# Attention with top-k masking and a routed MoE on one core: the gate's weights copied by ScalarE, and five constant tables moved to PSUM

## The chip, the cores and the metric

The kernel runs on one core of a Trainium2 chip. A core has five engines with queues of their own: TensorE (PE, matrix products and transposes), VectorE (DVE), ScalarE (ACT), GpSimd (POOL) and SyncE (SP, which here only issues DMAs). Each works through its instructions in the order of the program and waits on semaphores where it needs another's result. The metric is the device time of one execution in microseconds; less is better. SBUF is the working memory; PSUM holds 8 banks of 512 fp32 words in each of 128 partitions, and is where PE writes.

## The reference

The first part is attention in which each row keeps its 32 greatest scores, the second a mixture of eight experts, one per token:

```python
scores = scale * np.matmul(q, k.transpose(0, 1, 3, 2))          # B=8, H=8, S=576, D=64
kth = np.partition(scores, -32, axis=-1)[..., -32:-31]
scores = np.where(scores >= kth, scores, -1000000000.0)
attn = softmax(scores);  attn_out = np.matmul(attn, v)
x = attn_out.transpose(0, 2, 1, 3).reshape(B * S, H * D)        # 4608 tokens of 512

logits = x @ w_gate                                             # 8 experts
expert_idx = np.argmax(logits, axis=1)
gate_w = softmax(logits)[arange(N), expert_idx]
for e in range(8):                                              # each token goes to one expert
    out[mask_e] = gate_w[mask_e] * (np.maximum(x[mask_e] @ w1[e], 0) @ w2[e])
```

All inputs and the output are fp32.

## The kernel before

**Attention** runs over 144 steps `t` (line 1005 on), 18 for each of the 8 batches. A step handles two tiles of 128 query rows by 576 keys. The work on one pair of tiles is spread over several steps, and each pass of the loop issues, in this order:

- ACT: the exponentials of step t-4 (`exps`, line 468), which read the transposed scores from the PSUM tile `three` (named `tt`);
- ACT and POOL: the mask of step t-2 (`softmax`, lines 455 and 456): ACT writes the sign of score minus threshold, and POOL adds it to the scores so that masked ones vanish in the exponential;
- PE and ACT: the scores of step t+3 (`scores`, `scores_left`, lines 367 to 388) into PSUM, and their copy to SBUF (`sb`), from where SP also stores them to HBM (line 403);
- PE: the product with v of step t-5 (`av`, lines 478 and 493) and the transposes of step t-3 into `tt` (`transp`, line 462), nine chunks of 128 columns;
- DVE: the top-k of step t (`topk`): 21 MAX8 over pieces of the two tiles (line 1026) and then rounds of MAX8 and MATCH_REPLACE8 on the candidates (line 1034). POOL makes the thresholds `nb` of it (line 1008).

Beside this run small jobs, written as generators: `j_prep` (transposes of q and k), `j_sums`, `j_rows` (token rows and partial logits), `j_find` (rows whose mask kept a wrong number), `j_redo` and `j_patch` (these rows again) and `j_route` (expert and place of each token). They don't issue at once: `pe`, `act`, `vec` and `pool` (line 265 in the profile) put their instructions into four lists, `pq`, `aq`, `dq` and `gq`. A planner (`advance`, with costs from `need` and due times from `DUE`) decides at the end of each step which job goes on. PE's and ACT's lists are flushed in the next step ahead of the top-k; DVE's is flushed in the second half of the top-k, one job instruction behind each instruction of line 1034.

PSUM is full while attention runs: three banks for `tt` (of which the transposes use 1152 of 1536 columns), two for the scores, one (`px`) for the product with v and odd pieces, two for the jobs (`bank`, named `pt`). When attention ends (`att_open[0] = False`), all but the last two go to the MoE.

The tile framework sets the semaphores. Places that matter here: the prologue (lines 980 to 993) ends with two DVE copies that put the gate's weights `wg` into columns 128 to 143 of `turner`, the moving matrix with which `j_rows` turns token rows (first needed at step 14). `wg` comes by a DMA on SP's queue (line 129). Five constant tables in SBUF feed small DVE instructions: `level` (in `settle`, the softmax shifts), `idx1` (`j_find`, key), `slots` (`j_find`, `r_sl` and `r_qx`), `edesc` and `valid` (`j_route`).

**The MoE** (line 1084 on) gathers the tokens of an expert, splits them and the weights into two fp32r parts each, and multiplies on PE (lines 1154 and 1169). It starts with four experts' first tokens as soon as batch 4 is routed; the routes of the last batches run beside it.

Of the kernel before, what the change touches and what calls it, by code (L numbers as in the profile page):

```python
# [8 lines left out]
F32 = mybir.dt.float32  # L9
# [4 lines left out]
AF = mybir.ActivationFunctionType  # L14
OP = mybir.AluOpType
# [7 lines left out]
TOPK = 32  # L23
# [25 lines left out]
def attention_moe(ctx, tc, q, k, v, w_gate, w1, w2, out):  # L49
    nc = tc.nc  # L50
    B, H, S, D = q.shape
    HP = H // 2
    DM = H * D
    E = w_gate.shape[1]
# [17 lines left out]
    KB = MAIN + 1  # L72
# [23 lines left out]
    psum = att.enter_context(tc.tile_pool(name="psum", bufs=1, space=PSUM))  # L96
# [22 lines left out]
    turner = consts.tile([128, HP, RW], F32, name="turner")  # L119
# [8 lines left out]
    wg = consts.tile([128, DC, E], F32, name="wg")  # L128
# [6 lines left out]
    edesc = consts.tile([128, KB, E], F32, name="edesc")  # L135
    nc.gpsimd.iota(edesc, pattern=[[0, KB], [-1, E]], base=E, channel_multiplier=0,
                   allow_small_or_imprecise_dtypes=True)
    valid = consts.tile([128, KB, E], BF, name="valid")
# [3 lines left out]
    hist = consts.tile([128, E, 2 * KB + 1], BF, name="hist")  # L142
# [7 lines left out]
    idx1 = consts.tile([128, NLT], F32, name="idx1")  # L150
    nc.gpsimd.iota(idx1, pattern=[[1, NLT]], base=1, channel_multiplier=0, allow_small_or_imprecise_dtypes=True)
    slots = consts.tile([128, 128], BF, name="slots")
# [8 lines left out]
    stat = consts.tile([128, B, 3], F32, name="stat")  # L161
# [6 lines left out]
    for i in range(3):  # L168
        t = consts.tile([128, S], BF, name=f"sg{i}")
# [24 lines left out]
    level = consts.tile([128, 3], F32, name="level")  # L194
# [18 lines left out]
    for p in range(HP):  # L213
        for h in range(2):
# [3 lines left out]
            a = attr[:, t0:t0 + 2 * MAIN - 1:2, :]  # L218
# [4 lines left out]
            a = attr[h * LEFT:(h + 1) * LEFT, tl_, :]  # L223
# [8 lines left out]
    for i in range(3):  # L232
        t = work.tile([128, 2, KW], F32, name=f"qk{i}", bufs=1)
# [11 lines left out]
    for i in range(2):  # L245
        t = jobs.tile([128, NLT + 1, 2], F32, name=f"nb{i}", bufs=1)
# [3 lines left out]
    for i in range(NV):  # L250
        t = jobs.tile([128, 2, VW], F32, name=f"rv{i}", bufs=1)
# [5 lines left out]
    VQ, CNT, NB = {}, {}, {}  # L257
# [4 lines left out]
    cell, held, att_open = [1], [0], [True]  # L262

    def later(queue):
        return lambda f, *a, **k: queue.append(lambda: f(*a, **k))  # L265

    pe, act, vec, pool = later(pq), later(aq), later(dq), later(gq)
# [8 lines left out]
    def need(**k):  # L276
        return k

    def flush(queue):
        while queue:  # L280
            queue.pop(0)()
# [15 lines left out]
    def bank():  # L297
        return free.pop(0)

    NB9 = 2 * MAIN + 1  # L300
    three = psum.tile([128, NB9 * 128], F32, name="tt")

    MAINS = psum.tile([128, 2, 512], F32, name="ps")

# [132 lines left out]
    def spread(pt):  # L437
        pe(nc.tensor.matmul, pt[:, 0:128], top.to_broadcast([128, 128]), ident, start=True, stop=True)

    def settle(pt, ns, done):  # L440
        mm = jobs.tile([128, 1], F32, name="mm")
        vec(nc.vector.tensor_reduce, mm, pt[:, 0:128], axis=AX.X, op=OP.max)
        vec(done)
        k = len(ns)
        vec(nc.vector.scalar_tensor_tensor, shift[:, ns[0]:ns[0] + k], slope[:, None, :].to_broadcast([128, k, 3]), mm,
            level[:, None, :].to_broadcast([128, k, 3]), op0=OP.mult, op1=OP.add)

    SHIFTED = {0, 1, 2, 3}

# [165 lines left out]
    def j_find(b):  # L615
        sm = lambda name, shape, dt=F32: jobs.tile(shape, dt, name=name, bufs=1)
        yield need(dve=0.3)
        while (b + 1) * NLT // (2 * NT) - 1 not in CHECKED:
            yield
        key = sm("r_key", [128, NLT])  # L620
        vec(nc.vector.scalar_tensor_tensor, key, CNT[b], float(2 * TOPK - S), idx1, op0=OP.not_equal, op1=OP.mult)
        vec(nc.vector.max, rhs[:, :, 0], key)
        ok = sm("r_ok", [128, 9], BF)
        vec(nc.vector.tensor_scalar, ok[:, 0:8], rhs[:, :, 0], 0.0, None, op0=OP.is_gt, op1=OP.add,
            accum_out=ok[:, 8:9])
        nbb = NBB[b % 2]
        ntab = dram.tile([128 * (NLT + 1), 2], F32, name=f"ntab{b}")
        nc.sync.dma_start(ntab.rearrange("(p t) a -> p t a", p=128), nbb)
        yield need(spot=1, pe=0.1)
        pr, leave = spot("stat")  # L630
        pe(nc.tensor.matmul, pr[:, 0:1], before, ok[:, 8:9], start=True, stop=True)
        pe(nc.tensor.matmul, pr[:, 1:3], ones, ok[:, 7:9], start=True, stop=True)
        act(nc.scalar.activation, stat[:, b], pr[:, 0:3], AF.Copy)
        if 2 * b + 4 < NQ:
            spread(pr[:, 128:256])
            settle(pr[:, 128:256], [2 * b + 4, 2 * b + 5], leave)
            SHIFTED.update([2 * b + 4, 2 * b + 5])
        else:
            act(leave)
        yield need(slack=1)  # L640
        yield need(dve=1.3)
        sl = sm("r_sl", [128, 8], BF)
        vec(nc.vector.scalar_tensor_tensor, sl, slots[:, 0:8], stat[:, b, 0:1], ok[:, 0:8], op0=OP.add, op1=OP.mult)
        oh = sm("r_qx", [128, 512]).bitcast(BF).rearrange("p (j x) -> p j x", j=8)
        vec(nc.vector.tensor_tensor, oh, slots[:, None, :].to_broadcast([128, 8, 128]),
            sl[:, :, None].to_broadcast([128, 8, 128]), op=OP.is_equal)
        yield need(spot=1, pe=0.5)
        pl, leave = spot("li")
        for j in range(8):
            pe(nc.tensor.matmul, pl[:, 0:2], oh[:, j], rhs[:, j], start=(j == 0), stop=(j == 7))  # L650
        li = sm("r_li", [128, 2])
        act(nc.scalar.activation, li, pl[:, 0:2], AF.Copy)
        act(leave)
        yield need(slack=1)
        yield need(dve=0.1)
        fl = sm("r_fl", [128, 1], I32)
        vec(nc.vector.tensor_scalar, fl, li[:, 1:2], float(NLT + 1), li[:, 0:1], op0=OP.mult, op1=OP.add)
        yield need(pool=2.0)
        at = sm("r_at", [128, 4], I32)
        pool(nc.gpsimd.indirect_dma_start, out=at, out_offset=None, in_=atab,  # L660
             in_offset=bass.IndirectOffsetOnAxis(ap=fl[:, 0:1], axis=0))
        nb = jobs.tile([128, 8], F32, name="r_nb", bufs=3)
        pool(nc.gpsimd.indirect_dma_start, out=nb[:, 0:2], out_offset=None, in_=ntab,
             in_offset=bass.IndirectOffsetOnAxis(ap=fl[:, 0:1], axis=0))
        yield need(pool=1.8)
        qi = jobs.tile([128, 2], I32, name="r_qi", bufs=3)
        pool(nc.gpsimd.tensor_scalar, qi, at[:, 0:3:2], b * H * S, None, op0=OP.add)
        sb = jobs.tile([128, S], F32, name="r_sb", bufs=2)
        pool(nc.gpsimd.indirect_dma_start, out=sb, out_offset=None, in_=SCD[b],
             in_offset=bass.IndirectOffsetOnAxis(ap=at[:, 0:1], axis=0))  # L670
        hf = sm("r_hf", [128, 1])
        pool(nc.gpsimd.tensor_copy, hf, at[:, 1:2])
        hm = jobs.tile([128, H], F32, name="r_hm", bufs=3)
        pool(nc.gpsimd.tensor_scalar, hm, eight, hf, None, op0=OP.is_equal)
        hmb = hm[:, :, None].to_broadcast([128, H, D])
        pool(nc.gpsimd.tensor_scalar, used[:, b:b + 1], hf, float(H), None, op0=OP.is_lt)
        yield need(pool=0.7)

        low = nb[:, 2:3]
        pool(nc.gpsimd.tensor_scalar, nb[:, 3:4], nb[:, 1:2], 1.0 + 2.0 ** -10, None, op0=OP.mult)  # L680
        pool(nc.gpsimd.tensor_scalar, low, nb[:, 0:1], -(2.0 ** -7), None, op0=OP.mult)
        pool(nc.gpsimd.tensor_tensor, low, low, nb[:, 3:4], op=OP.add)
        FOUND[b] = (sb, nb, qi, hmb)
# [106 lines left out]
    def j_route(b):  # L790
# [14 lines left out]
        sh = small("sh", [128, KB, E])  # L805
        ex = small("gex", [128, KB, E])
        oh = small("oh", [128, KB, E])
# [2 lines left out]
        vec(nc.vector.tensor_reduce, lg, ll.rearrange("p i (h e) -> p i e h", h=H), axis=AX.X, op=OP.add)  # L810
        vec(nc.vector.tensor_reduce, mx, lg, axis=AX.X, op=OP.max)
        vec(nc.vector.tensor_tensor, sh, lg, mx[:, :, None].to_broadcast([128, KB, E]), op=OP.subtract)
        vec(nc.vector.scalar_tensor_tensor, oh, sh, 0.0, edesc, op0=OP.is_equal, op1=OP.mult)
        vec(nc.vector.tensor_reduce, fm, oh, axis=AX.X, op=OP.max)
        vec(nc.vector.tensor_tensor, oh, oh, fm[:, :, None].to_broadcast([128, KB, E]), op=OP.is_equal)
        yield need(dve=0.6)
        vec(nc.vector.tensor_tensor, hist[:, :, KB + 1:].rearrange("p e c -> p c e"), oh, valid, op=OP.mult)
        win = bass.AP(hist.tensor, hist.offset, [list(hist.ap[0]), list(hist.ap[1]), [1, KB + 1], [1, KB + 1]])
        vec(nc.vector.tensor_reduce, cum, win, axis=AX.X, op=OP.add)
        vec(nc.vector.tensor_copy, hist[:, :, KB], cum[:, :, KB])  # L820
# [22 lines left out]
        for c in range(KB):  # L843
            if c == 0 or b not in ahead or b == part_of[0][0]:
                yield need(pool=1.0)
            n = 128 if c < MAIN else LEFT
# [142 lines left out]
            for queue in (gq, pq, aq, dq):  # L989
                flush(queue)  # L990
    drain()
    for h in range(2):
        nc.vector.tensor_copy(turner[h * D:(h + 1) * D, :, 128 + h * E:128 + (h + 1) * E], wg[h * D:(h + 1) * D])
    nc.sync.dma_start(xs[0:PAD, :], zero[:, 0:DM])
    nc.sync.dma_start(atab.rearrange("(p t) a -> p t a", p=128), attr)
    for i in range(B):
# [8 lines left out]
    for t in range(steps + LAG + TD + 4):  # L1005
        n, s = divmod(t, NT)
# [26 lines left out]
        for m, (f, a) in enumerate(two):  # L1033
            f(*a)  # L1034
            if mine and m >= 2:
                mine.pop(0)()
        flush(mine)
        if t == 0:
            nc.vector.tensor_reduce(top, VQ[0][:, 0:2, 0], axis=AX.X, op=OP.max)
            first_pt = bank()  # L1040
            spread(first_pt)
            pq.pop()()
# [401 lines left out]
    n = over(moe_a, counts, cap, otab, lambda: next(g))  # L1444
# [50 lines left out]
```

## Time and profile before

| | us |
|---|---|
| median of 3 runs (lowest, highest) | 1278.51 (1277.42, 1278.90) |
| profiled execution: its own time | 1278.04 |
| profiled execution: its span, first to last instruction | 1276.2 |
| busy in the span: PE, DVE, POOL, ACT | 1209.7, 1020.9, 840.1, 832.6 |
| mean granted clock of PE | 0.988 |

A row of the timeline gives start, duration (us), engine, line, operation, output and inputs by the program's names, partitions x elements, and how many like it follow one another; in brackets stands the idle time of the engine before it and what ended this. PE is TensorE's matmuls, PEld its weight loads, SPq the DMAs that SP issues. Instructions of the small jobs all have line 265, so one goes by the tiles. A group's row gives count and durations of all instructions of one kind. The row of a stretch gives, for each engine, busy time and number of instructions, then the granted clock, the busy share of the DMA engines and GB/s.

### The profile page before, as it was taken

How to read it: one execution, taken by the hardware profiler on the slowest of the kernel's cores; microseconds unless marked ns; L12 is line 12 of the kernel's file. 1: busy time of each engine (PE TensorE's matmuls, PEld its weight loads, DVE VectorE, ACT ScalarE, POOL GpSimd, SP SyncE). 2: the span in 40 equal slices, each digit the busy share in tenths (PEclk: the TensorE clock that was granted, in tenths of full speed). 3: DMA queues.
4: the chain of work that ended last, by engine and by line, in shares of the span. 5: the costliest groups of instructions: out<-in, count | busy, mean ns of one | idle time of the engine just before them, and what ended most of it. 6: DMA issues, size and time to landing. Idle time of an engine off the chain costs nothing.

```text
span 1276.2 us, 31656 instructions
## 1 busy us (share of the span) xinstructions
PE 1209.7 (95%) x9126; PEld 963.3 (75%) x9126; DVE 1020.9 (80%) x6898; ACT 832.6 (65%) x1699; POOL 840.1 (66%) x1213
## 2 busy tenths in 40 slices
PE   6999999999999999999999879899999999999997
PEld 3667667766676767666667668789899998899996
DVE  7999999999999999999999986755674333446555
ACT  4999798998898898898998853333333232333433
POOL 4676666767977967967968858766554242455654
PEclk8999999999999999999999999899999999999999
DMA  6765564654655655665654635745665243556773
GB/s 172 233 179 184 165 204 145 191 180 154 190 177 165 196 169 167 194 176 164 187 172 144 184 101 147 223 125 173 167 192 162 75 135 93 155 164 193 228 213 112
DMA packets 276758, 215.37 MB, mean 169 GB/s; under 512 B 136617, under 2 KB 218713, under 8 KB 276576
## 3 DMA queue, kind: packets, MB, share of 16 engines
q1 hardware_dynamic: 265840, 190.11, 50.5%
q0 software_dynamic: 9504, 22.86, 5.7%
q8 instruction: 74, 1.21, 0.4%
q14 instruction: 108, 0.88, 0.2%
q10 hardware_dynamic: 1232, 0.30, 0.1%
HBM read 106.69 MB, written 107.90 MB: 168 GB/s over the span
## 4 chain that ended last, share of the span: by engine, by line
DVE 43%; PE 42%; ACT 5%; POOL 4%; issue 3%; DMA 2%; SPq 1%; POOLq 0%; ACTq 0%; DVEq 0%
DVE cand L1026 21%; PE ph L1154 17%; PE y L1169 17%; DVE cand L1034 9%; DVE vq L1034 8%; PE pt L265 2%; ACT sg L455 2%; POOL sb L456 2%; PE mt L1134 1%; PE px L478 1%; PE ps L367 1%; DVE xm L265 1%; POOL wl L958 1%; PE tt L462 1%; ACT sb L369 1%
## 5 line engine op out<-in xcount | busy, mean ns | idle before, releaser
L456 POOL TENSOR_TENSOR sb<-sb,sg 128x576 f32<-128x576 f32 x288 | 370.1, 1302 | 48.3 <-ACT sg L455 41.1
L1026 DVE MAX8 cand<-sb 128x8 f32<-128x52 f32 (+2 forms) x3024 | 366.3, 207 | 0.0
L958 POOL TENSOR_TENSOR wl<-r,wh 128x512 fp32r<-128x512 f32 x118 | 153.2, 1299 | 207.2 <-DVE wh L957 201.8
L455 ACT ACTIVATE sg<-sb,nb 128x576 int8<-128x576 f32 x288 | 229.0, 795 | 49.5 <-POOL sb L456 48.9
L1155 ACT ACTIVATE hh<-ph 128x256 fp32r<-128x256 f32 (+3 forms) x136 | 58.4, 429 | 247.6 <-PE ph L1154 247.5
L478 PEld LDWEIGHTS px<-et,rv 128*64 128x64 f32 x2688 | 129.9, 137 | 119.0 <-ACT xt L265 47.6
L1034 DVE MAX8 vq<-cand 128x8 f32<-128x22 f32 (+7 forms) x1152 | 200.5, 205 | 0.0
L367 PE MATMUL ps<-qk 64*128 64x512 f32 (+1 forms) x576 | 185.0, 650 | 3.9 <-ACT sb L369 3.2
L462 PE MATMUL tt<-turner,sb 128*128 128x128 f32 x1296 | 173.5, 276 | 14.8 <-POOL sb L456 10.4
L1156 DVE SCALAR_TENSOR_TENSOR hl<-ph,hh 128x256 fp32r<-128x256 f32 (+3 forms) x136 | 65.0, 478 | 150.8 <-ACT hh L1155 150.5
L468 ACT ACTIVATE et<-tt,shift 128x1152 f32<-128x1152 f32 x144 | 178.4, 1239 | 2.9 <-PE tt L462 2.9
L478 PE MATMUL px<-et,rv 128*64 128x128 f32 (+1 forms) x2688 | 163.1, 267 | 11.4 <-ACT xt L265 8.7
L1154 PE MATMUL ph<-xh,wh 128*128 128x256 f32 (+3 forms) x536 | 169.8, 317 | 0.0
L1154 PE MATMUL ph<-xh,wl 128*128 128x256 f32 (+3 forms) x536 | 165.8, 309 | 0.0
L1154 PE MATMUL ph<-xl,wh 128*128 128x256 f32 (+3 forms) x536 | 165.3, 308 | 0.0
L462 PEld LDWEIGHTS tt<-turner,sb 128*128 128x128 f32 x1296 | 145.8, 142 | 24.9 <-POOL sb L456 18.5
L1034 DVE MATCH_REPLACE8 cand<-vq,cand 128x22 f32<-128x22 f32 (+2 forms) x864 | 158.4, 189 | 0.0
L369 ACT ACTIVATE sb<-ps 128x1024 f32<-128x1024 f32 x144 | 149.1, 1036 | 8.7 <-PE ps L367 8.5
L1169 PE MATMUL y<-wh,hl 128*128 128x512 f32 x324 | 128.3, 396 | 1.4 <-DVE hl L1156 1.4
L1169 PE MATMUL y<-wl,hh 128*128 128x512 f32 x324 | 128.2, 396 | 0.0
L1169 PE MATMUL y<-wh,hh 128*128 128x512 f32 x324 | 128.2, 396 | 0.0
L1154 PEld LDWEIGHTS ph<-xh,wh 128*128 128x128 f32 x536 | 101.7, 190 | 4.2 <-issue 1.3
(260 smaller groups left out, 2178.4 us busy)
## 6 DMA issues: line engine op xcount, KB each, us to landing
r<-in_moe_w_dram SPq DMA_DIRECT2D x236, 256.0 KB
sc<-sb SPq DMA_DIRECT2D x128, 288.0 KB
sc<-sb SPq DMA_DIRECT2D x128, 256.0 KB
rv<-in_v_dram SPq DMA_DIRECT2D x32, 256.0 KB
xs<-xm SPq DMA_DIRECT2D x16, 512.0 KB
rq<-in_q_dram SPq DMA_DIRECT2D x60, 128.0 KB
rk<-in_k_dram SPq DMA_DIRECT2D x60, 128.0 KB
sc<-sb SPq DMA_DIRECT2D x32, 144.0 KB
```

Of the source, the lines that this page charges most:

```text
L367: nc.tensor.matmul(MAINS[:, n], qk[:, 0, w], qk[:, 1, 2 * LEFT:], start=True, stop=True)
L369: nc.scalar.activation(bass.AP(EX[-1].tensor, EX[-1].offset, [list(EX[-1].ap[0]), [S + LEFT, 2], [1, M]]), MAINS, AF.Copy)
L455: nc.scalar.activation(upper(SG[i]), SB[u], AF.Sign, bias=nb[:, i, 1:2], accum_out=CNT[b][:, 2 * lt + i:2 * lt + i + 1])
L456: nc.gpsimd.tensor_tensor(SB[u], SB[u], SG[i], op=OP.add)
L462: nc.tensor.matmul(tt[:, c], x[:, c * 128:(c + 1) * 128], ident, start=True, stop=True, is_transpose=True)
L468: nc.scalar.activation(ET[t], three.rearrange("p (c q) -> p c q", c=NB9), AF.Exp, bias=shift[:, t // NT, 0:1], scale=0.125)
L478: yield lambda kb=kb, blk=blk: nc.tensor.matmul(px[h * 64:(h + 1) * 64], block(rv, p % 2, kb if kb < MAIN else MAIN + n, h), et[:, blk, q] ...
L958: ((other or nc.gpsimd) if i else nc.vector).tensor_tensor(lo, r, hi, op=OP.subtract)
L1026: one[m][0](*one[m][1])
L1034: f(*a)
L1154: nc.tensor.matmul(ph, a[:, c, :], x[:, c, s], start=(m == 0), stop=(m == len(seq) - 1))
L1169: nc.tensor.matmul(PY[u, t], a[:, s], x, start=(f == 0 and m == 0), stop=(f == FC - 1 and m == 2))
```

## The change

Three things are edited. The tile `three` becomes the front of a tile `spare` that takes all three banks, and the columns behind it (1152 on, in the third bank, where the ninth chunk of the transposes lies) take fp32 copies of five tables. `const(name)` gives the copy while attention runs and the table in SBUF afterwards. ACT makes the copies: `level` in step 0, the others in step 4 (both flushed in the next step). The two copies of `wg` move from DVE at the end of the prologue to ACT behind step 3.

```diff
-    three = psum.tile([128, NB9 * 128], F32, name="tt")
+    spare = psum.tile([128, 3 * 512], F32, name="tt")
+    three = spare[:, 0:NB9 * 128]
+    TABLE = {}
+    o = NB9 * 128
+    for name, x in (("idx1", idx1), ("slots", slots), ("level", level), ("edesc", edesc), ("valid", valid)):
+        n = 1
+        for d in x.shape[1:]:
+            n *= d
+        y = spare[:, o:o + n]
+        TABLE[name] = (x, y if len(x.shape) == 2 else y.rearrange("p (a b) -> p a b", b=x.shape[2]))
+        o += n
+    assert o <= 3 * 512
+
+    def const(name):
+        return TABLE[name][1 if att_open[0] else 0]
...
         vec(nc.vector.scalar_tensor_tensor, shift[:, ns[0]:ns[0] + k], slope[:, None, :].to_broadcast([128, k, 3]), mm,
-            level[:, None, :].to_broadcast([128, k, 3]), op0=OP.mult, op1=OP.add)
+            const('level')[:, None, :].to_broadcast([128, k, 3]), op0=OP.mult, op1=OP.add)
...
-        vec(nc.vector.scalar_tensor_tensor, key, CNT[b], float(2 * TOPK - S), idx1, op0=OP.not_equal, op1=OP.mult)
+        vec(nc.vector.scalar_tensor_tensor, key, CNT[b], float(2 * TOPK - S), const('idx1'), op0=OP.not_equal, op1=OP.mult)
...
-        vec(nc.vector.scalar_tensor_tensor, sl, slots[:, 0:8], stat[:, b, 0:1], ok[:, 0:8], op0=OP.add, op1=OP.mult)
+        vec(nc.vector.scalar_tensor_tensor, sl, const('slots')[:, 0:8], stat[:, b, 0:1], ok[:, 0:8], op0=OP.add, op1=OP.mult)
...
-        vec(nc.vector.tensor_tensor, oh, slots[:, None, :].to_broadcast([128, 8, 128]),
+        vec(nc.vector.tensor_tensor, oh, const('slots')[:, None, :].to_broadcast([128, 8, 128]),
             sl[:, :, None].to_broadcast([128, 8, 128]), op=OP.is_equal)
...
-        vec(nc.vector.scalar_tensor_tensor, oh, sh, 0.0, edesc, op0=OP.is_equal, op1=OP.mult)
+        vec(nc.vector.scalar_tensor_tensor, oh, sh, 0.0, const('edesc'), op0=OP.is_equal, op1=OP.mult)
...
-        vec(nc.vector.tensor_tensor, hist[:, :, KB + 1:].rearrange("p e c -> p c e"), oh, valid, op=OP.mult)
+        vec(nc.vector.tensor_tensor, hist[:, :, KB + 1:].rearrange("p e c -> p c e"), oh, const("valid"), op=OP.mult)
...
     drain()
-    for h in range(2):
-        nc.vector.tensor_copy(turner[h * D:(h + 1) * D, :, 128 + h * E:128 + (h + 1) * E], wg[h * D:(h + 1) * D])
...
         flush(mine)
+        if t == 3:
+            for h in range(2):
+                r = slice(h * D, (h + 1) * D)
+                nc.scalar.activation(turner[r, :, 128 + h * E:128 + (h + 1) * E], wg[r], AF.Copy)
+        if t == 0:
+            act(nc.scalar.activation, const("level"), level, AF.Copy)
+        if t == 4:
+            for name in ("idx1", "slots", "edesc", "valid"):
+                act(nc.scalar.activation, const(name), TABLE[name][0], AF.Copy)
```

## The prediction

> **What bounds the kernel now.** I read the stages first: the busy time of each engine in four stretches (PE, PEld, DVE, ACT, POOL, then granted clock, DMA share and GB/s), then what VectorE (DVE) waited for, then the chain that ended last, by engine.
>
> ```profile
> 27.00:117.00 90.00, 86.94 (x743) 60.46 (x744) 86.86 (x784) 84.71 (x173) 59.74 (x77) 0.96 0.65 194
> 117.00:740.00 623.00, 587.25 (x5308) 430.62 (x5304) 623.00 (x5361) 550.03 (x1129) 477.98 (x716) 1.00 0.58 174
> ...
> 758.00:1277.00 519.00, 504.45 (x2892) 452.50 (x2892) 276.62 (x550) 177.21 (x360) 278.08 (x325) 0.99 0.54 160
> ```
>
> ```profile
> DVE turner L993 <- DMA wg<-in_moe_w_gate_dram: 6.9, 1, 6.9
> DVE mm L265 <- ACT stat L265: 3.1, 1, 3.1
> ```
>
> ```profile
> DVE 43%; PE 42%; ACT 5%; POOL 4%; issue 3%; DMA 2%; SPq 1%; POOLq 0%; ACTq 0%; DVEq 0%
> ```
>
> The chain is DVE's and then TensorE's (PE). From 117 to 740 us DVE is busy for all 623.00 us: a microsecond taken from it there is a microsecond of the kernel, unless it then has to wait. From 758 us PE is busy for 504.45 of 519 us and nothing of the change runs but SBUF reads as before, so a shift at 758 reaches the end whole. Before 117 us DVE stands still twice: 6.9 us for the gate's weights and 3.1 us for ScalarE's (ACT) `stat`. These two decide the first half of the change.
>
> **The start: the wait for `wg` goes, and the next wait takes it.**
>
> ```profile
> 10.00 0.27 ACT L388 ACTIVATE sb<-px 128x128 f32<-128x128 f32 x1
> ...
> 11.55 1.19 DVE L993 COPY turner<-wg 64x32 f32<-64x32 f32 x2 [6.89 <-DMA wg<-in_moe_w_gate_dram]
> 12.76 2.56 DVE L1026 MAX8 cand<-sb 128x8 f32<-128x52 f32 x21
> ...
> 24.75 1.03 PE L265 MATMUL pt<-turner,rq 128*128 128x128 f32 x2 [3.79 <-DMA rq<-in_q_dram]
> ...
> 27.09 0.60 ACT L265 ACTIVATE qk<-pt 128x512 f32<-128x512 f32 x1 [5.74 <-PE pt L265]
> ...
> 114.91 0.47 PE L265 MATMUL pt<-turner,top 128*128 128x128 f32 x2
> ...
> 116.49 0.18 ACT L265 ACTIVATE stat<-pt 128x3 f32<-128x3 f32 x1
> ...
> 116.71 0.29 DVE L265 TENSOR_REDUCE mm<-pt 128x1 f32<-128x128 f32 x1 [3.14 <-ACT stat L265]
> ```
>
> The first scores are complete at 10.00 + 0.27 = 10.27 us. Without the two copies the first MAX8 starts there and not at 12.76: DVE gains 2.49 us. But ACT's first sign pass stands in its queue behind the evacuation at 27.09 us, whose transposes on PE waited for the second load of q. That load is on SP's queue, which the change leaves as it is. So ACT, POOL and PE do not start earlier, and from 27 to 117 us ACT is busy for 84.71 of 90 us and PE for 86.94: they run at their own pace. DVE is ahead of them, and at `mm` (batch 0, step 21) it already waits 3.14 us for `stat`. With 2.49 us more lead it waits 2.49 us more. I count the start at **0**; its bounds are 0 and -2.49.
>
> ACT gets seven copies. `level` goes ahead of the evacuation at 27.09, into 5.74 us of idle time: 0 (some 0.2 us without that cover). The two of `wg` (64x32) and the four tables come at steps 3 and 5, in the busy stretch. No such copy is in the trace; the nearest are `stat` (128x3, 0.19) and `qk<-px` (64x128, 0.27):
>
> ```profile
> L265 ACT ACTIVATE stat<-pt x8: 152/191/193, 116.5 to 768.0; 128x3 f32<-128x3 f32 x8
> L265 ACT ACTIVATE qk<-px x64: 257/272/273, 6.8 to 686.4; 64x128 f32<-64x128 f32 x64
> ```
>
> Six by 0.27 is 1.6 us, the upper bound; zero is the lower, since ACT has 5.3 us of idle time there. I take **+0.9** at `stat`, and so at `mm`. No DMA is added or moved.
>
> **The new order: five tables in the bank of the transposes.** The tables lie behind the ninth transposed chunk, in the third bank of `tt`. The row of `mm` shows what this means. `mm` reads columns 128 to 255 of a bank that PE had written by 114.91 + 0.47 = 115.38; it still waited for `stat`, which only reads columns 0 to 2 of that bank. Two reads of one bank by two engines are put in program order. So each table read on DVE in step t stands behind ACT's exponentials and PE's transposes of that step, and the exponentials of step t+1 stand behind it, with the transposes, the signs and `stat` in line after them.
>
> The steady batch, from the timeline at 275 to 300 us (steps 53 to 57):
>
> ```profile
> 275.50 1.26 ACT L468 ACTIVATE et<-tt,shift 128x1152 f32<-128x1152 f32 x1
> 276.61 0.82 ACT L455 ACTIVATE sg<-sb,nb 128x576 int8<-128x576 f32 x1
> ...
> 279.26 0.18 DVE L265 SCALAR_TENSOR_TENSOR oh<-sh,edesc 128x40 f32<-128x40 f32 x1
> ...
> 279.40 1.29 ACT L468 ACTIVATE et<-tt,shift 128x1152 f32<-128x1152 f32 x1
> ...
> 282.34 2.51 POOL L456 TENSOR_TENSOR sb<-sb,sg 128x576 f32<-128x576 f32 x2
> ...
> 283.64 0.78 ACT L455 ACTIVATE sg<-sb,nb 128x576 int8<-128x576 f32 x1 [2.95 <-POOL sb L456]
> 284.25 0.81 DVE L265 TENSOR_TENSOR hist<-oh,valid 128x40 bf16<-128x40 f32 x1
> 284.90 0.77 PE L462 MATMUL tt<-turner,sb 128*128 128x128 f32 x5 [0.16 <-POOL sb L456]
> ...
> 297.24 0.19 ACT L265 ACTIVATE stat<-pt 128x3 f32<-128x3 f32 x1
> 299.59 0.28 DVE L265 TENSOR_REDUCE mm<-pt 128x1 f32<-128x128 f32 x1
> ```
>
> *What DVE saves.* `valid` at 284.25 lasts 0.81 us for 40 elements and ends just after POOL's add (282.34 + 2.51 = 284.85): it was held by POOL. The minimum of its group shows it free (durations are minimum, median, maximum in ns):
>
> ```profile
> L265 DVE TENSOR_TENSOR hist<-oh,valid x8: 321/802/5090, 284.2 to 878.1; 128x40 bf16<-128x40 f32 x8
> L265 DVE SCALAR_TENSOR_TENSOR oh<-sh,edesc x8: 170/188/2003, 279.3 to 874.4; 128x40 f32<-128x40 f32 x8
> L265 DVE SCALAR_TENSOR_TENSOR shift<-slope,mm,level x7: 231/352/756, 20.1 to 578.8; 128x6 f32<-128x6 f32 x6, 128x12 f32<-128x12 f32 x1
> L265 DVE SCALAR_TENSOR_TENSOR r_key<-cnt,idx x8: 184/185/186, 108.7 to 765.0; 128x36 f32<-128x36 f32 x8
> L265 DVE TENSOR_TENSOR r_qx<-slots,r_sl x8: 1207/1208/1224, 126.9 to 771.4; 128x1024 bf16<-128x1024 bf16 x8
> ```
>
> Four of the eight `valid` are held like this in the steady part, the first and the last of them in these stretches (busy time of that tile's instructions alone):
>
> ```profile
> 280.00:290.00 10.00, 0.81 (x1) 1.00 0.29 78
> ...
> 560.00:570.00 10.00, 0.80 (x1) 1.00 0.33 81
> ```
>
> They save 0.81 - 0.32 = 0.49 each: **-2.0**. `shift` goes to its 0.23: the longest, right behind `mm` of batch 0, saves 0.53, the other five 0.12 each: **-1.1**. `edesc`, `r_key` and `r_qx` have medians within 0.02 us of their minima: nothing holds them as a rule, 0.
>
> *What a read out of PSUM costs.* From the groups by shape, the first reads PSUM, the second SBUF only:
>
> ```profile
> L265 DVE TENSOR_TENSOR lp<-pt,rinv 128x48 f32<-128x48 f32 x32 | 6.3, 196 | 0.0
> L265 DVE TENSOR_TENSOR sh<-lg,mx 128x40 f32<-128x40 f32 x8 | 1.5, 192 | 0.1
> ```
>
> 196 ns for 48 elements against 192 for 40: no surcharge, 0. [...]
>
> *What the order costs.* `edesc` (step 53) ends at 279.44, so the exponentials that ran at 275.50 start 3.9 us later; `valid` (step 54) ends at 284.25 + 0.32 = 284.57, so those of 279.40 start 5.2 us later. Much of that falls into the 2.95 us in which ACT waits for POOL anyway. The sign pass follows the exponentials by 276.61 - 275.50 = 1.11 us, so at 285.7 and not 283.64: ACT is 2.07 us late. DVE notices at one place: `stat` would end at 297.24 + 0.19 + 2.07 = 299.50, while DVE, 0.49 earlier, reaches `mm` at 299.10. It waits 0.4 us in each of four batches: **+1.6**. The scores themselves are computed three steps ahead of DVE (LA = 3 in the code), so that side has room.
>
> *The end of attention.* Here one `valid` lasts the 5.09 us of its group's maximum, but the chain is POOL's:
>
> ```profile
> 738.86 1.21 ACT L468 ACTIVATE et<-tt,shift 128x1152 f32<-128x1152 f32 x1
> ...
> 744.06 0.19 DVE L265 SCALAR_TENSOR_TENSOR oh<-sh,edesc 128x40 f32<-128x40 f32 x1
> ...
> 745.70 4.97 POOL L456 TENSOR_TENSOR sb<-sb,sg 128x576 f32<-128x576 f32 x4
> ```
>
> The exponentials of 738.86 must now wait for `edesc` at 744.25. The sign pass after them ends 1.11 + 0.78 later, at about 746.2, and POOL's adds start there and not at 745.70. I take **+0.3**, between 0 and the whole 0.5 by which POOL starts later.
>
> **Sum:** 0 + 0.9 - 2.0 - 1.1 + 1.6 + 0.3 = -0.3 us. The profiled execution took 1278.04 us (span 1276.2), 0.5 below the median 1278.51 of the runs; on the median I predict **1278.2**.
>
> **Rivals.** *A, the start is kept:* ACT's and PE's pace turns out to follow DVE before 117 us and the copies hide. Then -2.49 is added and 0.9 falls away: -3.7, so **1274.8**. For it: DVE is busy for 86.86 of those 90 us. Against it: the 3.14 us at `mm`, which show DVE ahead.
>
> *B, slower, through `stat`:* PE is busy for 587 of 623 us and cannot make up what it loses when its transposes wait for the late exponentials. They ended at 284.90 + 0.77 = 285.67; behind exponentials that end at 284.57 + 1.29 = 285.86 (five took 0.77, so nine some 1.1) they end at 287.0, 1.3 us later. If that adds to ACT's 2.07, the lag is 3.37 and `mm` waits 3.37 - (299.59 - 297.43) + 0.49 = 1.7 us in four batches, 6.8 in place of 1.6: +4.9 in all, **1283.4**. It begins to cost at a lag of 2.16 - 0.49 = 1.67 us. For it: no idle time in ACT's line after 283.64; against it: POOL's adds set PE's pace there.
>
> *C, PSUM reads are dearer:* by the widest gap between rows of one operation, `shift` at 231 ns against `r_key` at 184, each of the 36 reads costs 0.047 us more, 1.7 in all: **1279.9**. The pair of `lp` and `sh` speaks against it. [...]
>
> **Chances.** Forecast 0.55 (own range 1275.5 to 1281), A 0.19, B 0.17, C 0.09. A measurement of this kernel tells 0.2%, some 2.6 us, from no change. Of the forecast 0.06 falls below that and 0.05 above; A is faster, B slower, C splits 0.06 to 0.03. Faster 0.25, same 0.50, slower 0.25. The range 1274.2 to 1283.6 takes in A and B.
>
> **What would show it.** The wait for `wg` gone and MAX8 starting near 10.3; waits of 5 us or more in batch 0 before 117 us, at `mm` or at `r_key`, which now also stands behind the transposes of its step; `valid` at 0.3 and `shift` at 0.23; exponentials waiting for DVE; `mm` waiting some tenths for `stat` in batches 2 to 5. I am wrong if DVE has no longer wait before 117 us (A), if `mm` waits over a microsecond in each batch (B), or if the tables' readers grow by 0.05 (C).

## The result and the profile after

The changed kernel takes 1290.74 us (median of 4 runs, 1289.30 to 1291.63) against 1277.97 us beside it (4 runs): 1.0101 of the time before, 95% interval 1.0083 to 1.0118, so slower by some 12.8 us. The profiled execution took 1291.63 us, with a span of 1289.8. The line numbers are the new ones: MAX8 L1038 and L1046, the exponentials L482, the transposes L476, the sign pass L469, POOL's add L470.

First what VectorE (DVE) waited for: total, times, longest, in us.

```profile
DVE mm L265 <- ACT stat L265: 10.7, 5, 2.4
DVE shift L265 <- ACT tt L265: 3.5, 1, 3.5
DVE r_key L265 <- PE pt L265: 1.7, 1, 1.7
```

The wait for `wg` is gone; `mm` waits for `stat` five times and not once. Four of these waits are of 2.27 to 2.38 us, in batches 2 to 5. The steady batch, from the timeline, answers to the stretch shown of before:

```profile
281.02 0.20 DVE L265 SCALAR_TENSOR_TENSOR oh<-sh,tt 128x40 f32<-128x40 f32 x1
281.25 1.22 ACT L482 ACTIVATE et<-tt,shift 128x1152 f32<-128x1152 f32 x1 [3.58 <-DVE oh L265]
282.62 2.15 PE L476 MATMUL tt<-turner,sb 128*128 128x128 f32 x9 [2.54 <-ACT et L482]
286.03 0.32 DVE L265 TENSOR_TENSOR hist<-oh,tt 128x40 bf16<-128x40 f32 x1
303.24 0.29 DVE L265 TENSOR_REDUCE mm<-pt 128x1 f32<-128x128 f32 x1 [2.27 <-ACT stat L265]
```

ACT's exponentials stand behind the read of `edesc`, and PE's transposes stand behind the exponentials. The third row holds one thing more: nine transposes take 2.15 us. Before, the same nine took 1.15:

```profile
277.89 1.15 PE L462 MATMUL tt<-turner,sb 128*128 128x128 f32 x9
```

The windows of PE in these microseconds (length, busy time, number of instructions, granted clock, DMA share, GB/s), first after, then before:

```profile
279.00:282.41 3.41, 1.08 (x26) 1.00 0.30 105
282.41:285.82 3.41, 3.20 (x15) 0.50 0.20 77
```

```profile
282.00:284.00 2.00, 2.00 (x26) 1.00 0.04 9
284.00:286.00 2.00, 1.84 (x16) 1.00 0.00 0
```

Behind the standstill of 2.54 us PE runs at half its clock (0.50) for 3.41 us.

Where the time went is read from the start of `mm` in each batch. The table has it for all profiled executions: `mm` of batch 0; the time from `mm` of batch 1 to that of batch 5, which is four steady batches; and what is left from there to the end of the span.

| kernel | time over before [95%] | `mm`, batch 0 | batches 1 to 5 | rest |
|---|---|---|---|---|
| before | 1 | 116.71 | 371.29 | 697.9 |
| after | 1.0101 [1.0083, 1.0118] | 118.92 | 380.77 | 700.7 |
| wg_only | 1.0003 [0.9994, 1.0012] | 118.12 | 371.11 | 696.3 |
| tables_only | 1.0125 [1.0109, 1.0140] | 117.14 | 380.63 | 702.7 |
| all_but_edesc | 1.0044 [1.0032, 1.0056] | 118.34 | 372.57 | 700.8 |
| edesc_only | 1.0120 [1.0105, 1.0135] | 117.65 | 380.28 | 704.8 |
| valid_only | 1.0035 [1.0022, 1.0049] | 117.31 | 372.95 | 697.8 |
| all_but_level | 1.0121 [1.0105, 1.0136] | 118.13 | 379.67 | 700.5 |
| read_early | 1.0013 [1.0004, 1.0022] | 116.97 | 371.42 | 698.5 |
| read_mid | 1.0074 [1.0056, 1.0091] | 117.48 | 373.90 | 701.1 |
| read_late | 1.0122 [1.0106, 1.0137] | 117.85 | 380.49 | 704.0 |
| read_end | 1.0200 [1.0176, 1.0225] | 116.51 | 387.57 | 704.1 |
| pe_block | 1.0043 [1.0026, 1.0060] | 116.93 | 372.88 | 699.5 |
| clock_kept | 1.0075 [1.0063, 1.0087] | 118.26 | 374.73 | 702.1 |
| after_again | 1.0129 [1.0109, 1.0150] | 118.62 | 379.37 | 704.6 |

From before to after: +2.2 at `mm` of batch 0, -0.9 over batch 1, +9.5 over the four steady batches, +2.8 in the rest: 13.6 us of span. The last column of one kernel (after, after_again) differs by 3.9 us between two executions, so single values in it tell little.

### The profile page after: what moved, and what is told of

It is laid out like the page before. It is cut to its first block, busy times and chain, and to the rows that moved or that the text cites. A ratio compares the mean times of both kernels' runs of the same rounds, so it can differ in the third digit from the quotient of the medians.

```text
span 1289.8 us, 31647 instructions
## 1 busy us (share of the span) xinstructions
PE 1211.0 (94%) x9126; PEld 970.8 (75%) x9126; DVE 1017.1 (79%) x6896; ACT 835.1 (65%) x1706; POOL 837.4 (65%) x1213
## 4 chain that ended last, share of the span: by engine, by line
PE 47%; DVE 39%; ACT 7%; issue 3%; DMA 1%; POOL 1%; SPq 1%; POOLq 0%; ACTq 0%; DVEq 0%
DVE cand L1038 19%; PE ph L1175 17%; PE y L1190 16%; DVE cand L1046 8%; DVE vq L1046 8%; PE pt L265 4%; PE ps L381 3%; PE tt L476 2%; ACT sg L469 2%; PE px L492 2%; ACT et L482 2%; ACT sb L383 2%; PE mt L1155 1%; DVE xm L265 1%; POOL wl L972 1%
## 5 line engine op out<-in xcount | busy, mean ns | idle before, releaser
L470 POOL TENSOR_TENSOR sb<-sb,sg 128x576 f32<-128x576 f32 x288 | 367.1, 1286 | 88.5 <-ACT sg L469 82.2
L1038 DVE MAX8 cand<-sb 128x8 f32<-128x52 f32 (+2 forms) x3024 | 366.4, 207 | 5.4 <-ACT sb L383 5.4
L469 ACT ACTIVATE sg<-sb,nb 128x576 int8<-128x576 f32 x288 | 228.4, 793 | 15.6 <-POOL sb L470 15.1
L482 ACT ACTIVATE et<-tt,shift 128x1152 f32<-128x1152 f32 x144 | 177.7, 1234 | 39.1 <-DVE oh L265 24.5
L1046 DVE MAX8 vq<-cand 128x8 f32<-128x22 f32 (+7 forms) x1152 | 200.5, 205 | 0.0
L476 PE MATMUL tt<-turner,sb 128*128 128x128 f32 x1296 | 172.0, 279 | 24.0 <-ACT et L482 19.2
L476 PEld LDWEIGHTS tt<-turner,sb 128*128 128x128 f32 x1296 | 149.2, 145 | 28.6 <-issue 20.0
L1046 DVE MATCH_REPLACE8 cand<-vq,cand 128x22 f32<-128x22 f32 (+2 forms) x864 | 158.5, 189 | 0.0
```

The costliest lines, as they stand in the source:

```text
L469: nc.scalar.activation(upper(SG[i]), SB[u], AF.Sign, bias=nb[:, i, 1:2], accum_out=CNT[b][:, 2 * lt + i:2 * lt + i + 1])
L470: nc.gpsimd.tensor_tensor(SB[u], SB[u], SG[i], op=OP.add)
L476: nc.tensor.matmul(tt[:, c], x[:, c * 128:(c + 1) * 128], ident, start=True, stop=True, is_transpose=True)
L482: nc.scalar.activation(ET[t], three.rearrange("p (c q) -> p c q", c=NB9), AF.Exp, bias=shift[:, t // NT, 0:1], scale=0.125)
L1038: one[m][0](*one[m][1])
```

## The experiments

### Which part of the change: wg_only, tables_only

wg_only keeps the two copies on ScalarE and reads all tables from SBUF:

```diff
-        return TABLE[name][1 if att_open[0] else 0]
+        return TABLE[name][0]
...
-        if t == 0:
-            act(nc.scalar.activation, const("level"), level, AF.Copy)
-        if t == 4:
-            for name in ("idx1", "slots", "edesc", "valid"):
-                act(nc.scalar.activation, const(name), TABLE[name][0], AF.Copy)
```

> The copies of the gate's weights stand on ScalarE behind the third step, as in the changed kernel; all five tables are read from SBUF throughout, so no table is copied. Theory O (the loss comes from the order of accesses in the bank of the tables): the first MAX8 starts near 10.1 us, `mm` of batch 0 waits 3.1 + 2.5 = some 5.6 us for `stat` and comes at 116.7 to 117.2 us, and there is no wait for `stat` at `mm` in batches 2 to 5; the time stays within 1 us of the kernel before (1277 to 1279). Rival S (the loss is in the start: copies on ScalarE that make its whole line late): `mm` of batch 0 at 118.9 as in the changed kernel and a time of 1280 or more. Rival A of the prediction (the start is kept): 1275.5.

tables_only puts the two copies of `wg` back ahead of the first step, on DVE, and keeps the tables in PSUM:

```diff
     drain()
+    for h in range(2):
+        nc.vector.tensor_copy(turner[h * D:(h + 1) * D, :, 128 + h * E:128 + (h + 1) * E], wg[h * D:(h + 1) * D])
...
-        if t == 3:
-            for h in range(2):
-                r = slice(h * D, (h + 1) * D)
-                nc.scalar.activation(turner[r, :, 128 + h * E:128 + (h + 1) * E], wg[r], AF.Copy)
```

> The copies of the gate's weights are back on VectorE ahead of the first step, as in the kernel before; the five tables lie in PSUM as in the changed kernel. Theory O: `mm` waits 2.3 us for `stat` in batches 2 to 5 as in the changed kernel, and of the 2.2 us at `mm` of batch 0 at least the part of the four table copies and of `r_key`'s wait stays: 1288 to 1291. Rival S: what the copies of the weights cost goes: 1280 to 1284.

Measured: 1.0003 and 1.0125 of before. The whole loss comes with the tables, and the move of `wg` neither gains nor costs anything that can be measured. The start of wg_only went as theory O said but for a later `mm` of batch 0 (118.12, not 117.2), which waited 4.5 us and not 5.6. Its lead is given back at `stat` (a wait of DVE, then ACT's timeline):

```profile
DVE mm L265 <- ACT stat L265: 4.5, 1, 4.5
```

```profile
28.03 0.60 ACT L265 ACTIVATE qk<-pt 128x512 f32<-128x512 f32 x1 [5.83 <-PE pt L265]
36.42 0.46 ACT L1053 ACTIVATE turner<-wg 64x32 f32<-64x32 f32 x2
```

The evacuation that stood at 27.09 before stands at 28.03: +0.94, and the copies take 0.46, together the 1.4 us by which `mm` is late. The 0.94 isn't the change's: over the fifteen profiled executions that row stands anywhere from 26.93 (read_early, with the same copies) to 28.03.

### Which table: all_but_edesc, edesc_only, valid_only, all_but_level

Each is the changed kernel with a shorter list of the tables that are copied to PSUM and read there; for all_but_edesc:

```diff
-        return TABLE[name][1 if att_open[0] else 0]
+        return TABLE[name][1 if att_open[0] and name in ('idx1', 'slots', 'level', 'valid') else 0]
...
-            for name in ("idx1", "slots", "edesc", "valid"):
+            for name in ('idx1', 'slots', 'valid'):
```

> The changed kernel with `edesc` alone back in SBUF. Theory O with its cause in `edesc` (the exponentials three steps behind the scores wait 3.6 to 5.4 us for it, PE stands still 2.5 us, and `stat` comes 4 us late): the lag at `stat` falls to under 1.7 us, `mm` waits 0 to 0.4 us in batches 2 to 5 instead of 2.3, and 8 us of the 12.8 go: 1282 to 1284. Rival V (`valid` sets the lag, as the prediction's sum had it, 2.07 us, and more behind it): `mm` still waits some 2 us and the time is 1288 to 1290. Rival N (each table read costs alike): a fifth to a quarter of the loss goes, 1287.5.

> `edesc` alone in PSUM, the other four tables in SBUF, the copies of the gate's weights on ScalarE. Theory O with its cause in `edesc`: `mm` waits 1.5 to 2.3 us in batches 2 to 5, and the time is 1284 to 1288. Rival V: no wait at `mm`, 1277 to 1279. Rival N: a fifth to a quarter of the loss, 1281.

> `valid` alone in PSUM, the other four tables in SBUF, the copies of the gate's weights on ScalarE. By the run with all but `edesc` in PSUM: the hold by POOL moves from `valid` to a neighbour (`po` 0.2 to 0.8 us), ACT waits up to 5 us for `hist` but `stat` is not late enough, +0.3 us in each steady batch and +3 at the end of attention: 1280 to 1283. Rival (the prediction's sum for `valid`, -2.0 us, holds once `edesc` is out of the way): 1275 to 1277.

> The changed kernel with `level` alone back in SBUF, and so without the copy of `level` on ACT. Theory (the start is set by ACT's line: its first sign passes and the copies that stand in it, while DVE's wait for `level` at step 1 only takes up DVE's lead): `shift` of step 1 no longer waits 3.5 us, `mm` of batch 0 waits that much more and comes at the same 118 to 119 us; time 1289.5 to 1291.5. Rival (DVE's 3.5 us at step 1 are what makes batch 0 late): `mm` of batch 0 at about 116.5 and a time of 1287 to 1288.

Measured: 1.0044, 1.0120, 1.0035 and 1.0121. `edesc` alone brings the whole loss, and more than the 1284 to 1288 us that were expected; without it the four steady batches take 372.57 us, 1.3 more than before and not 9.5. Rival N (each read costs alike) and rival V (`valid` sets the lag) fall. The parts do not simply add up: all_but_edesc still loses 0.44% by itself. What the exponentials, the transposes and `mm` waited for between 200 and 580 us, first with `edesc` alone, then with `valid` alone:

```profile
ACT et L482 <- DVE oh L265: 15.5, 4, 3.9
PE tt L476 <- ACT et L482: 11.4, 4, 2.8
DVE mm L265 <- ACT stat L265: 5.5, 3, 1.8
```

```profile
ACT et L482 <- DVE hist L265: 20.1, 4, 5.0
PE tt L476 <- ACT et L482: 7.2, 5, 1.7
DVE mm L265 <- ACT stat L265: 0.7, 3, 0.3
```

`valid` makes ACT wait longer (5.0 us against 3.9), but PE shorter (1.7 against 2.8), and `mm` follows PE. The exponentials that wait for `valid` are those behind which ACT stood 2.95 us for POOL before.

all_but_level answers for the start. In the changed kernel DVE waits 3.5 us at `shift` for ACT's copy of `level`. With `level` in SBUF that wait is gone, and `mm` of batch 0 still comes 90.9 us behind ACT's evacuation (27.22 to 118.13), where it came 91.1 us behind it (27.78 to 118.92); the time is no better. So ACT's line sets the start, not DVE's.

### The read or its place: read_early, read_mid, read_late, read_end

All tables lie in SBUF. DVE gets one extra copy of one element out of the third bank of `tt` in each step that reads `edesc`, at four places of the step. For the late place, right behind `edesc`:

```diff
         vec(nc.vector.scalar_tensor_tensor, oh, sh, 0.0, const('edesc'), op0=OP.is_equal, op1=OP.mult)
+        if clock[0] < steps:
+            vec(nc.vector.tensor_copy, peek, spare[:, 3 * 512 - 1:3 * 512])
```

The early, middle and end places are in the loop over the second half of the top-k: ahead of its first instruction, ahead of its seventh, and behind its last. The copies are six, not five, in the trace: the sixth falls at the end of attention.

> The same five one-element copies, in the same five steps, but ahead of the second half of the step's top-k, some 2.5 us earlier: by the trace at about 277.5 us of step 53, where the exponentials of that step have just ended (277.7) and the next ones come at 280.3. Theory O: DVE waits 0.2 us or less for them, ACT does not wait, `mm` waits no more than in the kernel without the copies: 1277.5 to 1279.5. Rival N (each read of that bank costs alike, wherever it stands): as with the late copy, 1286 or more.

> The one-element copy out of the bank of the transposes on DVE (tables in SBUF, nothing uses its result), ahead of the seventh instruction of the second half of the top-k, between the early place (0.13% slower than before, ACT waited 1.14 us for the copy in step 53, PE not at all) and the late one (1.2% slower, ACT 4.01, PE 2.96). Theory O': what counts is how long PE stands at the transposes behind the waiting exponentials, and PE's line takes some 1.1 us of ACT's wait for nothing: ACT waits 2.4 to 3.0 us, PE 1.3 to 1.9, `mm` 0.4 to 1.2 us in batches 2 to 5, time 1.002 to 1.007 of before. Rival T (a threshold: the step is either caught up or lost): as with the early copy or as with the late one.

> All five tables in SBUF, the copies of the gate's weights on ScalarE, and one extra DVE copy of one element (128x1) out of the bank of the transposes right behind each of the five `edesc` of the steps with scores; nothing uses its result. Theory O (it is the place of the access in the order of the bank that costs, whatever is read): ACT's exponentials wait 3.6 to 5.4 us for that copy in each of these steps, `mm` waits about 2 us for `stat` in batches 2 to 5, and the time is 1286 to 1292, as with `edesc` alone in PSUM, less what the sixth `edesc`, at the end of attention, costs. Rival P (the operand in PSUM makes DVE's instruction or what follows it slow): five copies by 0.2 us, 1278 to 1279.

> The same one-element copy behind the last instruction of the step's top-k, some 1.2 us later than the late place. Theory O': ACT waits about 5.2 us, PE 4.1, `mm` 1.1 us longer than the 1.9 with the late copy, time 1.016 to 1.020 of before. Rival T: as with the late copy, 1.012.

The same place of step 53 to 54 in the four kernels, in this order:

```profile
277.08 1.22 ACT L485 ACTIVATE et<-tt,shift 128x1152 f32<-128x1152 f32 x1 [1.14 <-DVE peek L1053]
278.44 1.17 PE L479 MATMUL tt<-turner,sb 128*128 128x128 f32 x9
```

```profile
278.97 1.22 ACT L485 ACTIVATE et<-tt,shift 128x1152 f32<-128x1152 f32 x1 [3.06 <-DVE peek L1054]
280.34 1.17 PE L479 MATMUL tt<-turner,sb 128*128 128x128 f32 x9 [2.02 <-ACT et L485]
299.89 0.28 DVE L265 TENSOR_REDUCE mm<-pt 128x1 f32<-128x128 f32 x1
```

```profile
280.23 1.22 ACT L485 ACTIVATE et<-tt,shift 128x1152 f32<-128x1152 f32 x1 [4.01 <-DVE peek L265]
281.60 1.71 PE L479 MATMUL tt<-turner,sb 128*128 128x128 f32 x9 [2.96 <-ACT et L485]
302.27 0.29 DVE L265 TENSOR_REDUCE mm<-pt 128x1 f32<-128x128 f32 x1 [1.88 <-ACT stat L265]
```

```profile
280.68 1.22 ACT L485 ACTIVATE et<-tt,shift 128x1152 f32<-128x1152 f32 x1 [5.17 <-DVE peek L1058]
282.04 2.15 PE L479 MATMUL tt<-turner,sb 128*128 128x128 f32 x9 [4.13 <-ACT et L485]
303.37 0.29 DVE L265 TENSOR_REDUCE mm<-pt 128x1 f32<-128x128 f32 x1 [3.77 <-ACT stat L265]
```

Six copies of one element, 0.14 us each, make the kernel slower by 0.1, 0.7, 1.2 or 2.0%, by nothing but their place among DVE's instructions. So the loss is a matter of the order of accesses in the bank, not of the operand in PSUM. In the steady batches the early copy costs nothing: ACT waits 1.14 us for it (the expectation put these exponentials in the wrong step and had no wait), and PE not at all. About 1.1 us of ACT's wait is free, then PE's standstill grows one for one: 2.02, 2.96, 4.13. But `mm` does not follow in this way. It has no wait behind 2.02 us, 1.88 behind 2.96 and 3.77 behind 4.13: between the first two, 0.9 us more standstill cost 1.9 and the slack besides. Theory O' missed here: it had 0.4 to 1.2 us at `mm` for read_mid and 3.0 for read_end, whose four batches wait 2.80 to 4.34. The length of the transposes, 1.17, 1.71 and 2.15 us, shows what was missing in it: the clock. In batches 3 and 5 of read_mid it fell behind the same 2.02 us, and `mm` waited 0.22 there; in the batch shown and in batch 4 it did not fall, and `mm` did not wait.

The 1.0074 of read_mid is hardly made by `mm`. Its four steady batches take 2.6 us more than before; two of the four `r_key`, at 0.18 us before, now last longer, up to 1.04 us, in the author's reading held by POOL as `valid` was before (minimum, median, maximum in ns):

```profile
L265 DVE SCALAR_TENSOR_TENSOR r_key<-cnt,idx x8: 184/187/1036, 108.1 to 770.7; 128x36 f32<-128x36 f32 x8
```

And at the end of attention its sixth copy makes PE stand 4.51 us.

### PE's delay without the wait, and the clock: pe_block, clock_kept, after_again

pe_block makes PE late by work instead of by a standstill, with all tables in SBUF (`look` holds the steps two behind those of `edesc`):

```diff
+        if t in look:
+            for _ in range(12):
+                nc.tensor.matmul(spare[:, NB9 * 128:NB9 * 128 + 128], ident, ident, start=True, stop=True)
         if grp(t - LAG - TD):
             transp(t - LAG - TD)
```

> All five tables in SBUF, no extra read on DVE, the copies of the gate's weights on ScalarE. Instead PE does twelve extra matmuls (128x128, some 0.23 us each, 2.8 us together, into unused columns; nothing uses them) right ahead of the transposes that in the changed kernel wait for the exponentials behind `edesc`. Theory O' (the loss is PE's: 2.8 us late at these transposes, with no room to make it up): `mm` waits 1.5 to 2.5 us for `stat` in batches 2 to 5 and the time is 1.006 to 1.012 of before, with no standstill of ACT behind DVE. Rival L (the loss is ACT's line: the exponentials and signs that come late behind `edesc`): no more than 1.003.

```profile
278.05 2.84 PE L1037 MATMUL tt<-turner 128*128 128x128 f32 x24
280.73 1.15 PE L477 MATMUL tt<-turner,sb 128*128 128x128 f32 x9
299.60 0.19 ACT L265 ACTIVATE stat<-pt 128x3 f32<-128x3 f32 x1
299.82 0.29 DVE L265 TENSOR_REDUCE mm<-pt 128x1 f32<-128x128 f32 x1
```

The transposes start 2.7 us after where they would by DVE's line (they stand 6.41 us behind the step's first MAX8, and 3.73 in wg_only), and `stat` ends at 299.79, just ahead of `mm`. No wait: theory O' missed its 1.5 to 2.5 us here. Of the 2.7 us only 2.2 reach `stat` (it ends 25.47 us behind that MAX8, and 23.26 in wg_only), and they use up just the slack: in wg_only `mm` starts 2.2 us behind the end of `stat`. The time, 1.0043, lies between both theories; again it is a neighbour of POOL's that lasts longer, `shift` with a median of 0.75 us for 0.35:

```profile
L265 DVE SCALAR_TENSOR_TENSOR shift<-slope,mm,level x7: 231/750/757, 18.4 to 580.5; 128x6 f32<-128x6 f32 x6, 128x12 f32<-128x12 f32 x1
```

In the changed kernel the transposes stand 6.74 us behind that MAX8, only 0.33 more, and `mm` waits 2.27.

clock_kept is the changed kernel with work for PE in the standstill, ahead of the leftover scores:

```diff
+        if t in look:
+            for _ in range(8):
+                nc.tensor.matmul(LEFTS, ident, ident, start=True, stop=True)
         scores_left(grp(t + LA))
```

> The changed kernel, with eight extra matmuls (128x128, some 0.24 us each, 1.9 us together, into columns of the bank of `px` that are written over next; nothing uses them) ahead of the leftover scores in the steps in which PE stands still behind `edesc`. ACT waits for `edesc` as before. Theory C (half of the loss in a steady batch is PE's clock: it falls to half after a standstill of 2.5 us and PE needs 1.6 us more for the next 3.5 us of work): PE's standstill falls from 2.5 to 0.6 us, the transposes behind it take 1.15 us and not 2.15, the granted clock stays at 1.00, `mm` waits 0.5 to 1.0 us in batches 2 to 5 instead of 2.3, and the time falls by 5 to 8 us to 1.004 to 1.006 of before. Rival O' (the standstill itself is what costs, the clock does not matter): `mm` waits 2 us or more and the time stays at 1.009 to 1.012, or above it for the extra matmuls.

> The changed kernel once more, beside clock_kept on the same chip: 1.008 to 1.013 of before by both theories.

```profile
280.59 1.22 ACT L483 ACTIVATE et<-tt,shift 128x1152 f32<-128x1152 f32 x1 [3.58 <-DVE oh L265]
281.96 1.17 PE L477 MATMUL tt<-turner,sb 128*128 128x128 f32 x9 [0.75 <-ACT et L483]
301.08 0.29 DVE L265 TENSOR_REDUCE mm<-pt 128x1 f32<-128x128 f32 x1 [0.78 <-ACT stat L265]
```

ACT waits the same 3.58 us as in the changed kernel. The granted clock stays at 1.00 (its window from 200 to 580 us: 1.00, after: 0.98), the transposes take 1.17 us, and `mm` waits 0.78 and not 2.27. The kernel takes 1.0075 of before, beside 1.0129 for the changed kernel on the same chip; by the ratios that is 0.5% less, some 7 us, though PE does 2 us more work in each of these batches. The gain is as theory C had it; the time itself stays above its 1.004 to 1.006. By the table, 1.5 us of what is left stand at `mm` of batch 0, 3.4 in the four steady batches and 4.2 behind them.

after_again shows it without any edit, by chance. Its first two steady batches, in PE's windows and in the rows of `mm`:

```profile
282.00:284.00 2.00, 1.69 (x15) 1.00 0.02 4
...
377.50:379.50 2.00, 2.00 (x16) 0.50 0.38 138
```

```profile
301.43 0.29 DVE L265 TENSOR_REDUCE mm<-pt 128x1 f32<-128x128 f32 x1 [0.78 <-ACT stat L265]
...
396.73 0.29 DVE L265 TENSOR_REDUCE mm<-pt 128x1 f32<-128x128 f32 x1 [2.32 <-ACT stat L265]
```

In the first the clock did not fall behind a standstill of 2.54 us, and `mm` waited 0.78; in the second it fell, and `mm` waited 2.32. all_but_level has the same pair: `mm` waits 0.77 us in batch 2, where the clock stayed up behind a standstill of 2.84 us, and 2.32 to 2.34 in batches 3 to 5, where it fell. The clock is 1.5 us of each of the longer waits.

## Why the prediction was wrong

The forecast was 1278.2, the range 1274.2 to 1283.6; the time is 1290.74. By its steps:

- **The start, 0: right, though DVE's lead went elsewhere.** The first MAX8 starts at 10.11 (10.27 forecast). The prediction had the 2.49 us come back at `mm` of batch 0, which would wait 3.14 + 2.49 = 5.6 us. It waits 1.4 there; DVE waits 1.7 at `r_key`, and 3.5 already at `shift` in step 1, which stands behind the copy of `level`. That copy was costed at 0 by the 5.74 us of ACT's idle time, with no look at who waits for it. all_but_level shows that it costs no time in the end.
- **ACT's copies, +0.9: too small, without weight.** Those of `wg` take 0.46, those of the tables stand from 44.27 to 45.29, so 1.5 us, near the upper bound of 1.6. With 0.69 from a later load of q, they are the 2.2 us at `mm` of batch 0.
- **`valid`, -2.0: right for the instruction, wrong for DVE.** It takes 0.32 as forecast. It reads PSUM at 286.03 and is done at 286.34, inside an add of POOL (285.36 to 286.63). But POOL's hold passes to a neighbour: the first held `po` ends at 308.98, an add of POOL at 308.93. The groups of `po<-po,ebase` (minimum, median, maximum in ns), before and after:

```profile
L265 DVE TENSOR_TENSOR po<-po,ebase x8: 184/192/239, 304.7 to 887.2; 128x40 f32<-128x40 f32 x8
```

```profile
L265 DVE TENSOR_TENSOR po<-po,ebase x8: 186/522/815, 308.2 to 900.8; 128x40 f32<-128x40 f32 x8
L265 DVE SCALAR_TENSOR_TENSOR shift<-slope,mm,tt x7: 202/203/226, 22.2 to 589.6; 128x6 f32<-128x6 f32 x6, 128x12 f32<-128x12 f32 x1
L265 DVE SCALAR_TENSOR_TENSOR r_key<-cnt,tt x7: 178/182/193, 112.6 to 677.1; 128x36 f32<-128x36 f32 x7
```

  Some 0.6 us in the held cases, against 0.49 saved. valid_only is 0.35% slower than before, and in no run with `valid` in PSUM are the steady batches shorter. (Of the 3 us that valid_only was expected to lose at the end of attention, 1.6 show, from `mm` of batch 5 to the MoE's first product.)
- **`shift`, -1.1, and the PSUM reads, 0: right.** `shift` takes 0.20; `r_key` 0.182 (0.185 before), `r_qx` 1.215 (1.208). The others stand at 0.197 (`edesc`, 0.188 before) and 0.217 (`r_sl`, 0.234). So none of the tables' readers grew by 0.05, and rival C falls. Its 36 reads are those of the five tables on DVE from 117 to 740 us: six each of `level` and `r_key`, seven each of `r_sl` and `r_qx`, five each of `edesc` and `valid`.
- **The order of accesses, +1.6: this step failed.** The mechanism was right: exponentials behind table reads (3.58 us behind `edesc` in the batch shown), `stat` late, and `mm` waiting (2.27 us there) once the lag had used up its slack. The four waits are 9.3 us. What failed is "much of that falls into the 2.95 us in which ACT waits for POOL anyway" as the measure of the cost. For ACT it holds: from 200 to 580 us it waits 15.2 us for `edesc`, 4.4 for `valid` and 6.7 for POOL, 26.3 together, and 26.1 for POOL alone before. But the transposes behind the exponentials of `edesc`'s step were not followed: PE stands still for 2.5 to 2.8 us there, where it did not before, and that uses up the 2.2 us of slack ahead of `mm`. The lateness alone is 0.8 us at `mm`, as clock_kept and the batches without a fall of the clock show, and the fall of the clock, of which the prediction has nothing, is another 1.5. The prediction took its 2.07 us (2.04 by its own rows) from `valid`, which alone costs `mm` 0.3.
- **The end of attention, +0.3: wrong by the same cause.** The prediction saw that the exponentials would wait for `edesc`, but put the cost at the start of POOL's adds and looked no further.

```profile
757.29 1.22 ACT L482 ACTIVATE et<-tt,shift 128x1152 f32<-128x1152 f32 x1 [5.38 <-DVE oh L265]
758.65 2.15 PE L476 MATMUL tt<-turner,sb 128*128 128x128 f32 x9 [5.31 <-ACT et L482]
760.91 0.34 DVE L265 TENSOR_TENSOR hist<-oh,tt 128x40 bf16<-128x40 f32 x1 [2.03 <-PE tt L476]
772.73 0.38 PE L1175 MATMUL ph<-xh,rv 128*128 128x256 f32 x1 [0.79 <-ACT xh L1156]
```

  PE stands 5.31 us and goes on at half its clock (0.50 from 754 to 762 us); then `valid`'s reader waits 2.03 for the transposes. The last row is the MoE's first product, at 757.45 before: +15.3, of which `mm` of batch 5 had 10.8, so 4.4 us are lost here. That the rest from this row on then took 1.7 us less (517.1 against 518.8) is within what it differs by between the fifteen executions, 516.6 to 519.9.

Rival B had the right place (PE cannot make up late transposes) and the right sign, for the wrong table: it delayed the transposes behind `valid` by 1.3 us and so came to 1.7 us at `mm`; it was given 0.17. Rival A fell with wg_only: the start is not kept. The prediction's own test, "`mm` waits over a microsecond in each batch (B)", is what the trace shows.

tables_only, with the four table copies, has `mm` of batch 0 at 117.14, only 0.4 us late, and that is in part the clock's doing. From ACT's evacuation near 27 us to `mm`, read_end and pe_block take 89.3 us, with a granted clock of 0.92 from 27 to 50 us; wg_only and the other three runs with an extra read run the same instructions up to there (some of the six with one memset more) and take 90.0 to 90.3, at 0.79 to 0.83. That puts, as an estimate, 0.7 to 1.0 us on the clock there; tables_only has 0.91, and the changed kernel 0.79.

Left open: the rest column was not taken apart for each kernel.

## What to carry to other kernels

A small operand in a PSUM bank that a pipeline between other engines uses put its reader into that pipeline's order here: ACT waited 3.58 us for a read of 0.20 us, and PE 2.54 us behind ACT. Cost such an operand by the place of the read in its own engine's line, and follow the wait through every engine behind it to the one whose slack it uses up (2.2 us ahead of `mm` here), not only through the first. Ask of each standstill of PE what clock it will have afterwards: behind the 2.54 us it was 0.50 for 3.41 us. And the hold by POOL wasn't removed by taking its victim away: `valid` went from 0.81 to 0.32 us, and the median of `po` from 0.19 to 0.52. Look which instruction is next.

## What the runs showed of the hardware

PE's granted clock is 1.00 or 0.50 in the traces of before and after. Within each of the two all its changes, 9 and 17, lie whole multiples of 3.41 us apart, and from 60 us on a stretch at half lasts 3.41 or 6.83 us before, 3.41 or 10.24 us after (the last one of each trace is cut off by its end). Take all points of a trace that lie such multiples away from a change as marks. The two windows shown with the result lie between marks: batch 2's standstill of 2.54 us (280.08 to 282.62) leaves PE busy for 1.08 us of the window ahead of the mark at 282.41, and the clock falls. In all_but_level a longer standstill in the same batch, 2.84 us (279.84 to 282.68), is split between two windows of the same length; both keep more work, and the clock stays up:

```profile
277.72:281.13 3.41, 2.12 (x44) 1.00 0.62 229
281.13:284.55 3.42, 1.87 (x17) 1.00 0.01 2
```

In the traces of before and after, from 60 us on, the clock fell behind all eleven windows between neighbouring marks in which PE, at full clock, was busy for at most 1.46 us, behind one of the eleven with 1.89 to 2.22 us (2.02 us, before, from 147.25 to 150.66 us), and behind none with more (busy times are the profile's, whose ends of matmuls are modelled). The length of a single standstill alone does not tell whether it falls: in valid_only it fell (0.50 from 288 to 290 us) behind 1.66 us, and in all_but_level it stayed up behind 2.84 us. In the changed kernel five falls in a row, from 282.41 us on, stand 95.57 us apart, 28 times 3.41 us, and `mm` comes every 95.3 us from batch 2 on, so a mark comes at nearly the same place of every batch.
